# Group 3's query transposes moved from TensorE to the DMA crossbar, its queries loaded ahead of its keys

## The chip, the cores and the metric

The kernel runs on one core of one Trainium2 chip. The metric is the time of one execution on the device in microseconds (us). TensorE is called PE below, VectorE DVE, ScalarE ACT, GpSimd POOL and SyncE SP, as in the profile.

## The reference

Windowed attention with four "sink" tokens, and behind it a gated feed-forward block on the same tokens:

```
scores = scale * q @ k.T                  # 4 batches, 8 heads, 768 tokens, head size 64
keep   = (key < 4) | (0 <= query - key < 128)
a      = softmax(where(keep, scores, -1e9))
x      = (a @ v) as 3072 tokens x 512
out    = (silu(x @ w_gate) * (x @ w_val)) @ w_out     # 512 -> 1536 -> 512
```

## The kernel before

**Tiling.** The 3,072 tokens are twelve groups of 256, three to a batch; group g is batch g // 3. Group 3 is thus the first group of the second batch. For attention, PE needs keys and queries with the head dimension along the partitions (tiles kT and qT, one of each per batch), while HBM holds them with tokens first, so each group's keys and queries have to be turned. `load_nat(g)` (line 106) loads them untouched into a tile `nat[g]` of 128 partitions, with four DMAs that POOL issues at line 113: two for the keys and then two for the queries, each 128 tokens by 512. Two routes turn such a block of 128 x 512:

- `step_TN(g, i, j, evict)` (line 273): four transposes on PE at line 279 into a PSUM tile `pn`, and one copy from there into kT or qT (i = 0 or 1) for token block j, by ACT (line 283) or DVE (line 285).
- `xbar(g, which)` (line 287): one DMA transpose a block at line 293, issued by SP, from `nat[g]` straight into kT or qT.

Group 2 and group 3 go by PE, groups 4 to 11 by the crossbar. Groups from 4 on share one single-buffered tile for `nat`; group 3's lies in a pool of three.

**The feed-forward** runs over eight token blocks tb of 256 or 512 tokens. A `gate` unit (line 611) is a projection into `pg` (line 564), a tanh on ACT (584), a projection into `pv` (564), and two DVE operations (592, and 598, 603 or 607). A `down` unit (line 644) is the last product into `pd` (657). They read xT, the turned attention output, which groups from 3 on get from another DMA transpose that SP issues (`step_X`, line 538).

**What sets the order.** The order is written out by hand: `weave` walks a list of units, and a dictionary hangs attention steps on them by the unit's number. In a `gate` unit, a step marked `ahead` stands before `pg`, and the others stand between `pg` and `pv`. Every engine takes its own instructions in that order. In the list that the change touches (from line 860), units 12 to 17 are the six gates of token block 2 and units 18 to 23 the downs of blocks 0 to 2. On it hang, among others: group 4's loads at unit 11; group 3's four `step_TN` at units 14 and 15; `xbar(4)` and group 5's loads at unit 15; group 3's scores (`S1(3)`, matmuls at line 382, the first readers of its kT and qT, marked ahead) at unit 17; group 3's PV products and group 4's scores at units 19 and 20, with the keys of `xbar(5)` and xT of group 3 on SP; then the rest of `xbar(5)` and xT of group 4.

**Queues.** SP issues, in this order: eight small loads `vcl` of sink values (line 211), the four transposes of `xbar(4)`, two of `xbar(5)`, two for xT of group 3, two of `xbar(5)`, two for xT of group 4. Every DMA issued by SP or ACT takes the next of eight semaphores in turn, and waits until the one that used that semaphore eight places before has landed; POOL's DMAs have eight of their own. POOL issues group 3's loads long before (they are in its program behind all the weights), then group 4's keys, queries and values, and group 5's once `xbar(4)` has landed, since that reads the single `nat` buffer.

Of the kernel before, what the change touches and what calls it, by code (L numbers as in the profile page):

```python
# [14 lines left out]
def kernel(  # L15
# [90 lines left out]
    def load_nat(g):  # L106
        b, c = divmod(g, GC)
        x = (natp if g > 3 else rowp).tile(
            [P, 2, 2, DM], BF16, tag="nat" if g > 3 else "rows", name="nat")
        for i, src in ((0, k), (1, q)):  # L110
            for j in range(2):
                t0 = c * 256 + j * P
                nc.gpsimd.dma_start(  # L113
                    x[:, i, j].rearrange("p (h d) -> p h d", d=D),
                    src[b, :, t0:t0 + P].rearrange("h p d -> p h d"))
        nats[g] = x
# [556 lines left out]
    def A(fn, *a):  # L673
        return lambda: fn(*a)

    def TN(g, evict="av"):
        return [A(step_TN, g, i, j, evict) for j in range(2) for i in range(2)]
# [126 lines left out]
    load_gate(2)  # L804
    step_vsb(0)
    load_nat(2)
    load_gate(3)
    load_v(2)
    load_gate(4)
    load_gate(5)  # L810
    for i in range(4):
        load_out(i)
    load_nat(3)
    load_v(3)
    nc.gpsimd.memset(vcl, 0.0)
# [41 lines left out]
    def NV(g):  # L857
        return L(A(load_nat, g), A(load_v, g))
# [3 lines left out]
        ((8, 8), PVs(2)[:2]), (9, [A(step_PV, 2, 0, 1, "a"), A(step_PV, 2, 1, 1, "a")]),  # L862
        ((10, 11), [A(step_X, 2, 0, "a"), ahead(A(step_X, 2, 1, "a"))]),
        (11, [NV(4), lambda: nc.gpsimd.tensor_copy(out=vcl[64:128], in_=vcl[0:64])]),
        ((14, 14, 15, 15), TN(3, "aa")),
        (15, [A(xbar, 4)]), (15, [A(load_nat, 5)]), (19, [A(xbar, 5, (0,))]),
        *one(17, 3), (18, [A(step_ks, 1)]), (18, [A(step_vsb, 1)]),
        ((19, 19, 19, 20), PVs(3)), (19, [S1(4)]), (20, [L(A(step_S2, 4), A(step_S3, 4))]), (20, Xs(3)), (20, [A(xbar, 5, (1,))]),
# [56 lines left out]
```

## Time and profile before

| | us |
|---|---|
| median of 3 runs | 233.52 (232.6 to 233.66) |
| the profiled execution | 233.03 |
| its span, first to last instruction | 231.2 |
| PE busy in the span | 226.0 (98%) |
| DVE, ACT, POOL busy | 151.1, 106.3, 84.8 |
| granted TensorE clock, mean | 1.000 |

The span is followed by engine. Where PE is busy all the time, whatever it no longer has to do comes off the time, and whatever it has to wait for is added. DMAs have no engine row of their own: an issue shows on the queue that made it (SPq, POOL), and its landing where the next instruction stops waiting. All positions below are in us from the span's start. "Landing" is the time of a DMA's last semaphore update in the trace.

### The profile page before, as it was taken

The page shows a single profiled execution, that of the slowest core. Times are in us where ns is not written, and L with a number is a line of the kernel's source. Part 1 is how long each engine was busy: PE and PEld are TensorE (multiplying, and loading weights), DVE is VectorE, ACT ScalarE, POOL GpSimd, SP SyncE. Part 2 cuts the span into 40 slices and gives each one's busy share as a digit, 9 for nine tenths or more (in the row PEclk, how much of TensorE's full clock was granted, in tenths as well). Part 3 has the DMA queues.
Part 4 walks back from the last instruction along what each step waited for, and adds up shares of the span by engine and source line. Part 5 has one row for each costly group of instructions (what it writes and reads, how often), then busy time and mean ns, then how long its engine had stood idle before and what let it go on. Part 6 is the DMA issues. An engine that isn't in the chain of part 4 may idle for free.

```text
span 231.2 us, 5467 instructions
## 1 busy us (share of the span) xinstructions
PE 226.0 (98%) x2171; PEld 126.8 (55%) x2171; DVE 151.1 (65%) x327; ACT 106.3 (46%) x212; POOL 84.8 (37%) x123
## 2 busy tenths in 40 slices
PE   7989999999999999999999999999999999999994
PEld 3669545786556854455454454454454544487443
DVE  5898888767650797960897960697960599778000
ACT  4784496367523827323626412735512823333221
POOL 8997965960500906904526064362000000000000
PEclk9999999999999999999999999999999999999999
DMA  7999999999998998998999999989814102000132
GB/s 134 164 188 178 179 199 206 163 155 125 154 168 211 80 132 103 145 197 124 134 124 118 147 87 203 144 107 131 94 48 136 48 0 45 3 0 0 69 116 91
DMA packets 112008, 28.04 MB, mean 121 GB/s; under 512 B 99056, under 2 KB 109040, under 8 KB 111984
## 3 DMA queue, kind: packets, MB, share of 16 engines
q0 software_dynamic: 79904, 14.29, 80.7%
q1 hardware_dynamic: 30672, 11.58, 28.5%
q10 hardware_dynamic: 1408, 1.84, 2.8%
q8 instruction: 17, 0.28, 0.5%
q14 instruction: 7, 0.06, 0.1%
HBM read 29.13 MB, written 6.29 MB: 153 GB/s over the span
## 4 chain that ended last, share of the span: by engine, by line
PE 93%; DMA 4%; DVE 1%; ACTq 0%; ACT 0%; issue 0%
PE pg L564 27%; PE pv L564 27%; PE pd L657 27%; PE o L494 3%; PE s L382 3%; DMA wg<-in_moe_w_gate_dram 3%; DMA st<-in_q_dram 2%; PE o L463 1%; PE pn L279 1%; PE o L454 1%; PE pk L432 1%; PE s L326 0%; PE px L543 0%; DVE kT L755 0%; PE pt L746 0%; PE s L765 0%
## 5 line engine op out<-in xcount | busy, mean ns | idle before, releaser
L592 DVE SCALAR_TENSOR_TENSOR u<-th,pg 128x512 bf16<-128x512 f32 x72 | 49.1, 683 | 45.3 <-ACT th L584 44.9
L564 PE MATMUL pg<-xT,wg 128*128 128x512 bf16 (+1 forms) x368 | 74.2, 333 | 0.5 <-DMA wg<-in_moe_w_gate_dram 0.5
L564 PE MATMUL pv<-xT,wv 128*128 128x512 bf16 (+1 forms) x368 | 74.1, 333 | 0.0
L584 ACT ACTIVATE th<-pg 128x512 f32<-128x512 f32 x72 | 43.8, 608 | 59.4 <-PE pg L564 59.2
L657 PE MATMUL pd<-wo,ht 128*128 128x512 bf16 (+2 forms) x300 | 65.9, 370 | 0.0
L564 PEld LDWEIGHTS <-wg 128*128 128x128 bf16 x368 | 35.2, 98 | 26.5 <-DMA wg<-in_moe_w_gate_dram 0.7
L564 PEld LDWEIGHTS <-wv 128*128 128x128 bf16 x368 | 34.6, 98 | 22.8 <-issue 0.2
L607 DVE TENSOR_TENSOR ht<-u,pv 128x512 bf16<-128x512 bf16 x60 | 41.2, 686 | 4.5 <-PE pv L564 0.4
L657 PEld LDWEIGHTS <-ht 128*128 128x128 bf16 x300 | 27.6, 98 | 28.4
L662 ACT ACTIVATE ot<-pd 128x512 f32<-128x512 f32 (+1 forms) x24 | 14.3, 595 | 50.2 <-PE pd L657 50.2
L395 ACT ACTIVATE e<-s 128x512 bf16<-128x512 f32 x54 | 28.5, 614 | 5.8 <-PE s L382 5.4
L113 POOL DMA_DIRECT2D nat<-in_k_dram x20 | 17.8, 896 | 28.6 <-DMA qT<-nat 27.1
L511 DVE TENSOR_TENSOR xn<-o,rcp 128x256 bf16<-128x256 f32 x45 | 17.9, 420 | 0.7
L128 POOL DMA_DIRECT2D vm<-in_v_dram x24 | 17.8, 772 | 1.1 <-DMA va<-in_v_dram 0.8
L113 POOL DMA_DIRECT2D nat<-in_q_dram x20 | 17.8, 908 | 1.0 <-DMA wg<-in_moe_w_gate_dram 0.8
L494 PEld LDWEIGHTS <-e 128*128 128x128 bf16 x256 | 11.5, 98 | 6.0 <-issue 0.2
L404 DVE TENSOR_TENSOR e<-e,maskq 128x768 bf16<-128x768 bf16 x24 | 13.1, 552 | 1.9 <-ACT e L395 1.9
L151 POOL DMA_DIRECT2D va<-in_v_dram x12 | 10.7, 921 | 4.5 <-DMA wo<-in_moe_w_out_dram 2.5
L703 POOL CAST warmed<-xT 1x1 f32<-1x1 bf16 x3 | 0.5, 175 | 28.5 <-DMA xT<-xn 28.5
L503 DVE RECIPROCAL rcp<-o 128x4 f32<-128x4 f32 x48 | 7.1, 171 | 4.8 <-PE o L494 4.5
L664 DVE TENSOR_SCALAR ot<-pd 128x128 f32<-128x128 f32 x1 | 0.3, 292 | 14.3 <-PE pd L657 14.3
L333 ACT ACTIVATE e<-s 128x512 bf16<-128x512 f32 x16 | 8.3, 625 | 0.3 <-PE s L326 0.3
(86 smaller groups left out, 141.4 us busy)
## 6 DMA issues: line engine op xcount, KB each, us to landing
out_dram<-ot SPq DMA_DIRECT2D x17, 256.0 KB
nat<-in_k_dram POOLq DMA_DIRECT2D x20, 128.0 KB, 4.2
nat<-in_q_dram POOLq DMA_DIRECT2D x20, 128.0 KB, 5.2
va<-in_v_dram POOLq DMA_DIRECT2D x12, 128.0 KB, 5.5
wg<-in_moe_w_gate_dram POOLq DMA_DIRECT2D x6, 256.0 KB, 7.1
wv<-in_moe_w_val_dram POOLq DMA_DIRECT2D x6, 256.0 KB, 7.6
wo<-in_moe_w_out_dram POOLq DMA_DIRECT2D x4, 384.0 KB, 11.1
out_dram<-ot ACTq DMA_DIRECT2D x6, 256.0 KB
```

The source lines that it names most:

```text
L113: nc.gpsimd.dma_start(x[:, i, j].rearrange("p (h d) -> p h d", d=D), src[b, :, t0:t0 + P].rearrange("h p d -> p h d"))
L128: nc.gpsimd.dma_start(vms[b][p0:p1, t - 1, :, 0:D], v[b, :, t0:t0 + p1 - p0].rearrange("h p d -> p h d"))
L395: nc.scalar.activation(e_t[g][:, e0:e0 + 512], pss[g][w, i], AF.Exp, scale=scale)
L404: nc.vector.tensor_tensor(e, e, m.broadcast_to([P, 2, 384]), op=ALU.mult)
L494: nc.tensor.matmul(o, l, r, start=(c == 0 and i == 0), stop=(i == len(mms) - 1), skip_group_check=True)
L511: nc.vector.tensor_tensor(xn, po[:, :, 0:D], rcp.broadcast_to([P, 4, D]), op=ALU.mult)
L564: nc.tensor.matmul(ps[:, i * n:(i + 1) * n], ws[fi][:, c, fo * P:(fo + 1) * P], xTs[tb][:, c], start=(c == 0), stop=(c == DMC - 1))
L584: nc.scalar.activation(th, pg, AF.Tanh, scale=0.5)
L592: nc.vector.scalar_tensor_tensor(u, th, 1.0, pg, op0=ALU.add, op1=ALU.mult)
L607: nc.vector.tensor_tensor(hts[tb][:, f:f + 512 // SIZES[tb]].rearrange("p a n -> p (a n)"), u, pv, op=ALU.mult)
L657: nc.tensor.matmul(po, hts[tb][:, f, ts * P:(ts + 1) * P], wos[f // n][:, f % n, lo:hi], start=(f == 0), stop=(f == DFC - 1))
L662: nc.scalar.activation(ot, po, AF.Copy, scale=0.5)
```

## The change

`load_nat(3)` loads the two query blocks first and the two key blocks behind them; all other groups keep keys first. On the list of units, group 3's queries go by `xbar(3, (1,))`, hung on unit 12, so SP issues their two DMA transposes ahead of `xbar(4)`. PE keeps the keys: one `step_TN` in unit 14 and one in unit 15, evicted by ACT. The order of instructions of the two kernels differs in nothing else: PE has 8 transposes fewer (4,344 to 4,328 rows, loads of weights counted), ACT two copies fewer, POOL two pairs of loads exchanged, SP two transposes more between `vcl` and `xbar(4)`.

```diff
@@ load_nat
-        for i, src in ((0, k), (1, q)):
+        for i, src in (((1, q), (0, k)) if g == 3 else ((0, k), (1, q))):
@@ the list of units
-        ((14, 14, 15, 15), TN(3, "aa")),
+        (12, [A(xbar, 3, (1,))]), ((14, 15), [A(step_TN, 3, 0, j, "aa") for j in range(2)]),
         (15, [A(xbar, 4)]), (15, [A(load_nat, 5)]), (19, [A(xbar, 5, (0,))]),
```

## The prediction

> **What bounds the kernel now.** I read the page first: the span is 231.2 us and PE is busy through all of it.
>
> ```profile
> span 231.2 us, 5467 instructions
> PE 226.0 (98%) x2171; PEld 126.8 (55%) x2171; DVE 151.1 (65%) x327; ACT 106.3 (46%) x212; POOL 84.8 (37%) x123
> PE   7989999999999999999999999999999999999994
> ```
>
> So PE work that goes comes off the time, and any wait of PE is added whole. Next I read the chain of work that ended last around group 3's transposes (start, us, what):
>
> ```profile
> 45.53 0.87 PE pg L564 x8
> 46.41 0.45 PE pn L279 x8
> ...
> 48.60 0.45 PE pn L279 x8
> ...
> 51.67 0.77 PE s L382 x18
> ```
>
> PE goes from one to the next without a gap: the longest idle of PE behind the first 16 us is under 0.15 us. The two rows of `pn` are the sixteen transposes of group 3, 0.45 us for each eight. The row `s` is S1(3), the first reader of what they made. Third is the timeline of SP, which has to make the queries instead, and what it waited for from 44 to 58 us (total, times, longest):
>
> ```profile
> 40.65 2.67 SPq L211 DMA_DIRECT2D vcl<-in_v_dram  x8
> 49.52 2.58 SPq L293 DMA_TRANSPOSE kT<-nat  x2
> 52.20 2.52 SPq L293 DMA_TRANSPOSE qT<-nat  x2
> ```
>
> ```profile
> SPq L293 <- DMA nat<-in_k_dram: 3.9, 1, 3.9
> SPq L293 <- DMA vcl<-in_v_dram: 2.3, 1, 2.3
> ```
>
> SP is free at 43.3, waits 2.3 us for the first of the `vcl` loads to land (45.62, by its semaphore), and 3.9 us more for group 4's keys. Last, the DMA engines from 45 to 55 us, in 40 slices of 0.25 us:
>
> ```profile
> DMA  9999999999999999999999999999999999999999
> GB/s 157 151 177 150 156 210 148 146 145 145 154 155 152 155 155 153 154 154 156 151 151 157 152 153 149 152 156 174 187 153 122 100 107 68 84 159 148 174 246 179
> ```
>
> They are full: POOL's loads of values and of group 4 stand in a backlog. From about 51.75 to 53.5 the bytes fall from 150 to 68 GB/s: that is `xbar(4)`'s first transpose running beside that backlog.
>
> **The change, part by part.**
>
> *PE.* Eight transposes go: 8 x 0.056 = 0.45 us (one row of eight). All of it is on the path, none beside other PE work. PE reaches S1(3) at 51.60 (its first matmul) - 0.45 = 51.15. Removed with them are two ACT copies of 0.605 us; ACT is busy 46% and no PE wait in this stretch ends at it, so I count them at nothing; nor can they give more, as PE has no idle time here.
>
> *Order of the loads.* POOL issues the same four loads at the same times, so the queries take the first places. By the semaphores those land at 43.54 and 44.51 and the other two at 45.47 and 46.34. The keys now take the latter; PE reads the first at 46.14 (unit 14) and the second at 48.2 (unit 15), 0.7 and 1.9 us late enough. Cost: nothing; if the first landed over 0.7 us later, the excess.
>
> *When SP issues.* The two new transposes stand behind `vcl`. The first needs the query block (43.54) and the semaphore of the first `vcl` load (45.62), so it goes at 45.64. An issue takes 1.22 to 1.27 us, so the second goes at about 46.95, and SP is free at 48.2, ahead of the 49.52 at which group 4's keys let `xbar(4)` begin. SP's own time thus delays nothing; if those keys came sooner, at most the 2.5 us of two issues.
>
> *When they land.* No transpose runs at 46 us before, so the duration comes from others. From issue to the last semaphore update: 2.45 us with nothing beside it (69.97 to 72.42). Pairs that met POOL's backlog (issue of the first, landing of the second, difference; POOL's packets beside each):
>
> ```
>  81.40 ->  87.28   5.88   2365, 1108   (the backlog ends in between)
>  49.52 ->  55.76   6.24   4538, 2863
>  94.96 -> 101.85   6.89   4391, 4131
> 110.91 -> 118.23   7.32   4356, 2648
> 123.22 -> 131.93   8.71   4792, 3334
> 142.47 -> 150.12   7.65   2372, 3061
> 155.65 -> 162.83   7.18   4297, 2707
> ```
>
> The backlog at 45.6 is as thick as in the last six (about 600 of POOL's packets each 0.5 us) and has nine more us to run. So I take their median, 7.25 us: the second lands at 45.64 + 7.25 = 52.89. S1(3) waits for both. PE stands 52.89 - 51.15 = **1.74 us**. The bounds: 5.88 gives a wait of 0.37; 8.71, and 1.0 more because the `vcl` loads are ahead on the same queue until 48.60, gives 4.2. What stands behind the waiting matmul is all of PE's work, so everything shifts by the same. Net so far: 1.74 - 0.45 = +1.29.
>
> *What the transposes cost POOL's loads.* In the dips at 52, 97, 99 and 126 us POOL's queue falls short of its rate by 0.7 to 1.15 us for each transpose that runs beside it; alone, a transpose takes 0.5 us (`xbar(4)` lands at 55.12, 55.76, 56.24 and 56.72, once the backlog is gone). Two more cost 1.0 to 2.3 us; I take 2 x 0.9 = 1.8. So `xbar(4)` lands at about 58.5; S1(4) needs it at 59.45 + 1.29: covered by 2.2 us. But group 5's load waits for it, and from there a tight chain runs: group 5's keys, two transposes, two for xT of group 3, two more, two for xT of group 4, all back to back on SP from 61.98 to 73.84. POOL and PE show its end:
>
> ```profile
> 57.27 1.75 POOL L113 DMA_DIRECT2D nat<-in_k_dram  x2 [6.22 <-DMA qT<-nat]
> ...
> 75.32 0.18 POOL L703 CAST warmed<-xT 1x1 f32<-1x1 bf16 x1 [14.54 <-DMA xT<-xn]
> ```
>
> xT of group 4 lands at 75.26, and PE reads it at 75.72: 0.46 us of cover. Late by 1.8, it comes at 77.06; PE, late by 1.29, asks at 77.01. That adds 0.05. Behind it the next link is group 6's queries (88.32, read at 89.15: 0.83 of cover), and from 103 us on xT and kT land 2 us and more ahead, so no more is added.
>
> **Sum:** 233.03 (the profiled execution: 231.2 of span and 1.8 around it) - 0.45 + 1.74 + 0.05 = **234.4 us**, +0.6%. The profiled execution lies 0.49 under the median of the runs; against that median the same sum would be 234.9, inside the range.
>
> **A rule against the change.** One transpose of 128 x 128 on PE costs 0.056 us of the path here, and its crossbar counterpart has 2.45 us as its shortest row. [...]
>
> **The rivals.**
>
> 1. *A short wait at S1(3), and xT of group 4 as the end.* If the pair lands as early as the shortest contended row, the wait is 0.37 and PE asks for xT at 75.64. With 1.0 to 1.8 us of delay it lands at 76.26 to 77.06: a wait of 0.6 to 1.4, and 233.6 to 234.4 us. For it: the order of waits is a matter of one us. Against it: six of seven contended pairs took longer. Chance 0.26.
> 2. *In time (not slower).* If the transposes run as without a backlog, the second lands at 46.95 + 2.45 = 49.4, 1.7 us ahead of PE. The point from which this holds is a pair in under 5.5 us. Then the time is 233.03 - 0.45 = 232.6, or up to 233.6 if POOL's loads still lose 1.0. For it: the rows without a backlog. Against it: no pair beside a backlog was that quick. Chance 0.14. [...]
> 3. *A long wait.* `vcl` ahead on the queue and a pair like that at 123 us: 55.4, a wait of 4.2, net +3.75, 236.8 us. Chance 0.08.
>
> **How the numbers follow.** The forecast has the remaining 0.52, with its own spread of about 234.2 to 235.5. A measurement of this kernel can tell about 0.5% (1.17 us) from no change. The forecast and the long wait lie nearly all above +1.17 (0.57 of 0.60); the short wait and in time nearly all within (0.40, with what the forecast leaves); no mechanism here gives more than 0.45 us back, so faster by over 0.5% has 0.02, for chance alone; slower 0.57, within 0.41. The range leaves out half of the long waits and most of "in time": 232.8 to 236.1.
>
> **What would show it.** In the changed kernel: two rows of `pn` with 0.22 us each; SP's new pair at 45.6 and 46.9; PE idle ahead of S1(3), released by DMA qT<-nat, at about 51.1 to 52.9; group 5's load at about 59 in place of 57.27; POOL's row for xT near 77. No idle at S1(3) makes the landing step wrong; idle there with no shift of group 5's load makes the cost to POOL's loads wrong; a wait at `pn` makes the loads' order wrong.

## The result: 2.8% slower

| | before | changed |
|---|---|---|
| median of 6 runs each, us | 233.18 (232.60 to 233.89) | 239.72 (238.83 to 240.52) |
| the profiled execution, us | 233.03 | 240.52 |
| its span, us | 231.2 | 238.7 |
| granted clock, mean over the span of the profiled execution | 1.000 | 0.986 |

The ratio is 1.0277, with a 95% interval of 1.0245 to 1.0310: +6.5 us between the medians. The forecast was 234.4 and its range ended at 236.1; the sign was right and the size was not.

The changed kernel's page shows a gap in PE's row that the kernel before has nowhere, and beside it something that no view of before had: a slice in which the granted clock, the share of its full rate that TensorE is given, is 5 tenths.

```profile
span 238.7 us, 5454 instructions
...
PE   7979999975999999999999999999999999999994
...
PEclk9999999995899999999999999999999999999999
```

The same row of the kernel before:

```profile
PEclk9999999999999999999999999999999999999999
```

The other five executions of the changed kernel have mean clocks of 0.984 to 0.993, so each of them had such a stretch too, whose place is not seen without a trace.

What ended PE's waits, over the whole span (total, times, longest; the second line is the start of the kernel, where PE went on 1.2 us later than in the profile of before; the kernels start alike, and in most of the other profiles this wait is 0.5 to 1.2 us):

```profile
PE s L382 <- DMA qT<-nat: 3.7, 1, 3.7
PE pg L564 <- DMA wg<-in_moe_w_gate_dram: 1.5, 1, 1.5
```

In the kernel before, the second line reads as follows, and the first has no counterpart:

```profile
PE pg L564 <- DMA wg<-in_moe_w_gate_dram: 0.5, 1, 0.5
```

The chain of work through this place (start, us, what), and the same stretch by stages (length, PE busy, then the other engines, granted clock, DMA share, GB/s):

```profile
48.12 7.89 DMA qT<-nat
56.00 0.14 issue
56.14 1.46 PE s L382 x18
57.60 1.82 PE pg L564 x8
59.42 1.71 PE pv L564 x8
61.13 3.74 PE pd L657 x16
```

```profile
52.00:54.50 2.50, 0.41 (x4) 0.12 (x2) 1.37 (x2) 0.17 (x1) 0.00 (x0) 1.00 2.71 138
54.80:56.10 1.30, 0.00 (x0) 0.00 (x0) 0.00 (x0) 0.00 (x0) 0.00 (x0) 0.50 2.02 150
56.20:61.50 5.30, 5.30 (x36) 3.67 (x37) 1.41 (x3) 3.62 (x7) 0.64 (x1) 0.50 0.94 88
61.70:65.00 3.30, 3.30 (x20) 1.58 (x19) 2.38 (x7) 0.60 (x1) 2.66 (x4) 1.00 1.26 80
```

The second transpose was issued at 48.12 and landed at 56.00; PE had stood since 52.42. When it went on, S1(3) took 1.46 us where it had taken 0.77, and the `pg` behind it 1.82 where it had taken 0.98: nearly twice as long. The stage from 56.2 to 61.5 shows why. PE is busy all of it at a clock of 0.50, and a busy row alone would not have told it. The clock records put the half clock from 54.77 to 61.59, 6.83 us, of which 5.45 had work to do.

Matched matmul by matmul, the two profiles differ by +1.24 us ahead of group 3 (the start), then -0.45 for the transposes (`pn` is now eight matmuls), +3.72 for the wait, +2.6 until the clock is back at 61.6, and nothing that grows behind that: together 7.1 of the 7.5 us between the spans, the rest standing behind the last matmul. Without the start that is 5.9, against 6.5 between the medians.

SP and POOL of the changed kernel:

```profile
46.71 2.61 SPq L293 DMA_TRANSPOSE qT<-nat  x2
49.74 2.60 SPq L293 DMA_TRANSPOSE kT<-nat  x2
52.44 3.16 SPq L293 DMA_TRANSPOSE qT<-nat  x2
```

```profile
60.86 1.75 POOL L113 DMA_DIRECT2D nat<-in_k_dram  x2 [9.58 <-DMA qT<-nat]
```

SP's new pair goes out first, as the list of units says, and its own issues delay the next ones by nothing (49.74 is when group 4's keys landed). Group 5's load goes 3.6 us later than before (60.86 for 57.27); 1.1 us of that is the later start, as POOL's first load of group 4 goes at 43.32 for 42.23.

### The profile page after: what moved, and what is told of

It reads as the page before. It is cut to its first block, busy times and chain, and to the rows that moved or that the text cites. A ratio compares the mean times of both kernels' runs of the same rounds, so it can differ in the third digit from the quotient of the medians.

```text
span 238.7 us, 5454 instructions
## 1 busy us (share of the span) xinstructions
PE 228.4 (96%) x2163; PEld 127.9 (54%) x2163; DVE 151.6 (63%) x327; ACT 105.7 (44%) x210; POOL 84.3 (35%) x123
## 4 chain that ended last, share of the span: by engine, by line
PE 78%; DMA 17%; POOL 1%; DVE 1%; issue 1%; SPq 1%; POOLq 0%
PE pd L657 26%; PE pg L564 21%; PE pv L564 20%; DMA wv<-in_moe_w_val_dram 7%; DMA wo<-in_moe_w_out_dram 4%; PE s L382 3%; DMA qT<-nat 3%; PE o L494 2%; DMA vcl<-in_v_dram 2%; PE w L730 1%; PE o L463 1%; PE pt L746 1%; PE pk L432 1%; SPq L293 1%; PE o L454 1%
## 5 line engine op out<-in xcount | busy, mean ns | idle before, releaser
L564 PE MATMUL pg<-xT,wg 128*128 128x512 bf16 (+1 forms) x368 | 75.0, 336 | 1.5 <-DMA wg<-in_moe_w_gate_dram 1.5
L564 PE MATMUL pv<-xT,wv 128*128 128x512 bf16 (+1 forms) x368 | 75.0, 336 | 0.0
L564 PEld LDWEIGHTS <-wv 128*128 128x128 bf16 x368 | 35.1, 99 | 23.1 <-issue 0.2
L395 ACT ACTIVATE e<-s 128x512 bf16<-128x512 f32 x54 | 28.5, 610 | 9.8 <-PE s L382 9.4
L494 PEld LDWEIGHTS <-e 128*128 128x128 bf16 x256 | 11.6, 98 | 6.1 <-issue 0.2
L382 PE MATMUL s<-qT,kT 64*64 64x64 bf16 (+4 forms) x366 | 8.5, 223 | 3.7 <-DMA qT<-nat 3.7
L382 PEld LDWEIGHTS <-kT 64*64 64x64 bf16 (+1 forms) x366 | 6.8, 108 | 7.3 <-issue 7.2
```

Of the source, the lines that this page charges most:

```text
L382: nc.tensor.matmul(pss[g][w, lo // 8][part, 64 * (lo % 8):64 * (lo % 8) + 64 * (hi - lo)], kTs[b][r, p, k0:k0 + kn], qTs[b][r, p, cc:cc + ...
L395: nc.scalar.activation(e_t[g][:, e0:e0 + 512], pss[g][w, i], AF.Exp, scale=scale)
L494: nc.tensor.matmul(o, l, r, start=(c == 0 and i == 0), stop=(i == len(mms) - 1), skip_group_check=True)
L564: nc.tensor.matmul(ps[:, i * n:(i + 1) * n], ws[fi][:, c, fo * P:(fo + 1) * P], xTs[tb][:, c], start=(c == 0), stop=(c == DMC - 1))
```

## The experiments

**Theory.** The loss is (a) the wait at S1(3), long because the transposes run beside POOL's backlog of loads, and (b) the half clock that came behind that wait (0.50 from 54.77 to 61.59), which the prediction had not priced. **Rivals:** the new order of the loads; the place behind `vcl` on SP; the delay of group 4's and 5's loads, with no part of the wait; transposes that are slow by themselves. The ratio of each kernel to before is given with its 95% interval.

**1. The order of the loads alone.** The kernel before with this line of the change:

```diff
-        for i, src in ((0, k), (1, q)):
+        for i, src in (((1, q), (0, k)) if g == 3 else ((0, k), (1, q))):
```

> Group 3's queries are loaded ahead of its keys, and PE turns both as before. If the order of the loads costs nothing, the time is that of before, 233.2 within 0.5. If the order is what costs (keys late for unit 14, or a shift in POOL's queue), PE waits at pn and the time goes towards 239.7.

Measured: 233.05 us beside 233.29, ratio 0.999 (0.996 to 1.001), and no PE wait at `pn`. The order costs nothing.

**2. The transposes without the wait.** As 1, and:

```diff
+        (12, [lambda: [nc.sync.dma_start_transpose(scratch[:, j], nats[3][:, 1, j]) for j in range(2)]]),
         ((14, 14, 15, 15), TN(3, "aa")),
```

> As e1_order, and SP also makes the two crossbar transposes of group 3's queries, at unit 12, into a tile that nothing reads: their DMA cost without a PE wait for them. If the cost is the wait at S1(3) and the slow clock behind it alone, 233.2. If it is the delay of POOL's loads and of the chain behind them (group 5's load at about 60 in place of 57.3, xT of group 4 about 2 to 3 us later than PE asks for it), 235 to 236, with an idle PE at about 75.7. If even the transposes' mere presence gives the whole loss, 239.7.

Measured: 236.15 beside 233.29, ratio 1.012 (1.006 to 1.018), full clock in the profile. S1(3) starts at 51.47, on time. The first transpose was issued at 45.59 and the second landed at 55.68. PE and POOL later; the first line is S1(5) in the kernel before, which does not wait:

```profile
74.58 0.89 PE L382 MATMUL s<-qT,kT 64*64 64x192 bf16 x52
```

```profile
75.91 0.83 PE L382 MATMUL s<-qT,kT 64*64 64x192 bf16 x45 [1.15 <-DMA qT<-nat]
```

```profile
91.94 0.84 PE L382 MATMUL s<-qT,kT 64*128 64x256 bf16 x18 [1.40 <-DVE ht L607]
```

```profile
60.15 1.75 POOL L113 DMA_DIRECT2D nat<-in_k_dram  x2 [8.94 <-DMA qT<-nat]
```

The two PE rows that wait are S1(5) and S1(6). Group 5's load is late by 2.9 us, its queries land at 75.78 (3.4 us late: 1.9 by the issue of the last transpose, 1.4 by its length), and group 6's at 91.80 (the profile names DVE for the second, but that had long been done; POOL's `turned(6)`, a step that waits for the same queries, is released at 91.92). So two transposes in this stretch cost 2.9 us even if nobody waits for them. In the changed kernel this cost is not seen, because PE is late by more: group 5's queries land at 76.20 there, and S1(5) starts at 81.72.

**3. PE kept busy through the wait.**

```diff
+        (17, [ahead(lambda: fill(17, bank([P, 512], FP32, "w"), 512))]),
         *one(17, 3),
```

> The changed kernel with 17 matmuls of 512 columns on zeros put ahead of S1(3), about 3.7 us of PE work in the place of the wait. The wait stays covered but costs its time. If the slow clock behind the idle stretch is a cost of its own, it is gone: granted clock 1.000 and 233.2 - 0.45 + 3.7 = 236.5. If the clock is a mark and no cost, 239.7 as the changed kernel.

Measured: 237.22 beside 233.29, ratio 1.016 (1.011 to 1.021). The wait is covered: the second block lands at 54.95, S1(3) starts at 55.08.

```profile
51.14 3.83 PE L730 MATMUL w<-zero 128*128 128x512 bf16 x17
55.08 0.84 PE L382 MATMUL s<-qT,kT 64*128 64x256 bf16 x18
```

```profile
55.00:60.00 5.00, 4.92 (x46) 3.32 (x47) 2.41 (x5) 3.54 (x7) 0.00 (x0) 1.00 1.38 113
60.00:65.00 5.00, 5.00 (x97) 2.87 (x96) 3.73 (x12) 2.17 (x5) 3.51 (x4) 1.00 0.91 100
```

With the same DMAs and nearly the same delay but no idle PE, the clock stays at 1.00 and the loss is 3.9 us in place of 6.5: the half clock is a cost of its own, some 2.6 us. Work of no use on PE made the changed kernel faster.

**4. `vcl` behind the transposes.**

```diff
-    load_sinks(vcl, 1, B)
...
-        (11, [NV(4), lambda: nc.gpsimd.tensor_copy(out=vcl[64:128], in_=vcl[0:64])]),
-        (12, [A(xbar, 3, (1,))]),
+        (11, [NV(4)]),
+        (12, [A(xbar, 3, (1,)), A(load_sinks, vcl, 1, B), lambda: nc.gpsimd.tensor_copy(out=vcl[64:128], in_=vcl[0:64])]),
```

> The changed kernel with the eight small vcl loads put behind the two transposes on SP, so that these go as soon as the queries have landed, about 2 us sooner. If the place behind vcl makes them late, they land in time: 232.8, no idle at S1(3). If the backlog of POOL's loads makes them slow, they still take 7 to 9 us from the first issue to the second landing, and PE waits about 1 to 2 us: 234 to 235 with the clock held, 236 to 238 if it falls all the same.

Measured: 237.36 beside 233.29, ratio 1.017 (1.011 to 1.023). Issued at 43.98, the pair lands at 53.20: 9.2 us again, so the place behind `vcl` is not what makes it long. The same length begun sooner leaves PE a wait of 1.61 us at S1(3), and there are 0.35 and 1.75 more at S1(4) and S1(5), in the profile:

```profile
PE s L382 <- DMA qT<-nat: 3.7, 3, 1.8
```

The profiled execution held the clock (mean 0.998) and took 237.38, over the forecast of 234 to 235 for that case by 2 us: the waits at S1(4) and S1(5) had been left out of it. The edit is part of their cause, since the `vcl` loads now stand ahead of `xbar(4)`, which SP issues at 53.57 in place of 49.74. The other three executions, with mean clocks of 0.986 to 0.992, took 237.16 to 238.44.

**5. The backlog taken away.** Group 4's loads (`NV(4)`: keys, queries and values) are held on POOL until the two transposes have landed, for which `turned(3)` waits.

```diff
-        (11, [NV(4), lambda: nc.gpsimd.tensor_copy(out=vcl[64:128], in_=vcl[0:64])]),
-        (12, [A(xbar, 3, (1,))]),
+        (11, [lambda: nc.gpsimd.tensor_copy(out=vcl[64:128], in_=vcl[0:64])]),
+        (12, [A(xbar, 3, (1,)), A(turned, 3), NV(4)]),
```

> The changed kernel with all of group 4's loads held on POOL until the two transposes have landed, so that these meet only group 3's last loads. If POOL's backlog makes the pair slow, it lands by about 51 (under 6 us in place of 9.3) and PE waits at S1(3) for 0.5 us at most, at full clock; group 4 is then late instead, with waits of 1 to 2 us at S1(4) and S1(5), 235 to 236. If the pair is slow by itself, the wait of 3.7 us and the slow clock stay, and the time is 239.7 or more.

Measured: 241.74 beside 233.65, ratio 1.035 (1.032 to 1.039). The pair is issued at 45.99 and 47.72 and lands at 49.47 and 50.20, the second in 2.48 us. S1(3) does not wait (first line below; the second is S1(4)):

```profile
51.60 0.84 PE L382 MATMUL s<-qT,kT 64*128 64x256 bf16 x18
```

```profile
65.71 1.50 PE L382 MATMUL s<-qT,kT 64*64 64x192 bf16 x52 [6.18 <-DMA qT<-nat]
```

So the backlog is what makes the pair long; the time is worse, since S1(4) then waits 6.18 us and the clock falls there (its 52 matmuls take 1.50 us for 0.89 before; mean clock 0.986). The forecast of 1 to 2 us for that wait was wrong: held until 50.5, group 4's loads ran beside its own four transposes, of which the first went at 53.81 for 49.52 before and the last landed at 65.57 for 56.72.

**6. A shorter gap.** As 3, with five of the matmuls.

```diff
-        (17, [ahead(lambda: fill(17, bank([P, 512], FP32, "w"), 512))]),
+        (17, [ahead(lambda: fill(5, bank([P, 512], FP32, "w"), 512))]),
```

> The changed kernel with 5 of the matmuls on zeros ahead of S1(3), so about 2.6 us of idle PE are left of 3.7. If the clock falls some 2.4 us after PE has stopped, as in the changed kernel's profile, it falls, and the time is about 239 to 239.7. If it takes an idle stretch of over 2.6 us, it holds, and the time is that with 17 of them, 237.2.

Measured: 238.92 (three runs: 239.04, 238.92, 237.03) beside 233.65, ratio 1.020 (1.016 to 1.025). In the profile PE stood 3.23 us, as the pair was longer than expected, and the clock fell 3.0 us after PE had stopped, for 3.41 us. The mean clock is 0.991 and 0.993 in the two runs at 239 and 0.998 in the run at 237.03.

**7. Early.** Group 3's loads stand ahead of the output weights on POOL, its transposes ahead of `vcl` on SP.

```diff
     load_gate(5)
+    load_nat(3)
     for i in range(4):
         load_out(i)
-    load_nat(3)
...
+    xbar(3, (1,))
     load_sinks(vcl, 1, B)
...
-        (12, [A(xbar, 3, (1,))]), ((14, 15)
+        ((14, 15)
```

> The changed kernel with group 3's loads ahead of the output weights' on POOL, and its two transposes ahead of vcl on SP: they go at about 38 to 39 and may take 9 us without PE waiting. If the wait and the clock were all, 232.8 (0.45 under before). If the two transposes also delay POOL's loads for group 4 and, through the single nat buffer, group 5 by about 2.9 us, waits of 1 to 1.5 us at S1(5) and S1(6) stay: 235 to 236.

Measured: 235.70 beside 233.65, ratio 1.009 (1.006 to 1.012). The pair is issued at 36.11 and lands at 47.61, 3.8 us ahead of S1(3), which does not wait. Group 5's load is late by 2.35 us. Its last query transpose goes 1.1 us later than before (71.06 for 69.97), and takes 5.33 us in place of 2.45, with four stores of the output in flight beside it in place of two; S1(5) waits:

```profile
76.53 0.89 PE L382 MATMUL s<-qT,kT 64*64 64x192 bf16 x52 [2.02 <-DMA qT<-nat]
```

**8. Early, and a buffer of its own for group 5.**

```diff
-        x = (natp if g > 3 else rowp).tile(
-            [P, 2, 2, DM], BF16, tag="nat" if g > 3 else "rows", name="nat")
+        own = g in (2, 3, 5)
+        x = (rowp if own else natp).tile([P, 2, 2, DM], BF16, tag="rows" if own else "nat", name="nat")
```

> As e8_early, and group 5 is loaded into a free buffer of group 3's pool, so that its load need not wait until xbar(4) has landed. If that wait is the path by which the delay reaches PE, the waits at S1(5) and S1(6) go: 232.8, or 0.2% under before. If the transposes slow whatever stands in the backlog, group 5's load just joins it, and 234 to 236 remains.

Measured: five runs of 235.89 (the profiled one), 237.00, 237.98, 239.47 and 240.09, at mean clocks of 1.000, 0.993, 0.993, 0.986 and 0.986; ratio 1.014 (1.010 to 1.018) for the three quickest. Group 5's load goes at 55.07 with no wait for a landing, and S1(5) and S1(6) do not wait. But its packets now stand beside `xbar(4)`, whose last transpose lands at 61.82 in place of 56.72, and S1(4) waits:

```profile
61.95 0.89 PE L382 MATMUL s<-qT,kT 64*64 64x192 bf16 x52 [2.53 <-DMA qT<-nat]
```

The wait moved; it did not go.

**9. Group 4's values out of the backlog**: in the early kernel, in the kernel before as a control, and in the changed kernel.

```diff
-        (11, [NV(4), lambda: nc.gpsimd.tensor_copy(out=vcl[64:128], in_=vcl[0:64])]),
+        (11, [A(load_nat, 4), lambda: nc.gpsimd.tensor_copy(out=vcl[64:128], in_=vcl[0:64])]),
...
-        (15, [A(load_nat, 5)]),
+        (15, [A(load_nat, 5), A(load_v, 4)]),
```

> As e8_early, and group 4's five value loads stand behind group 5's keys and queries on POOL, so they wait until xbar(4) has landed and are no part of the backlog that it meets. If that backlog is what makes group 5 late, xbar(4) lands by about 57, group 5's queries are there when S1(5) asks, and the values (asked for at 64.3) are in time by a little: 232.8 to 233.5. If any two more transposes here cost their time whatever stands around them, a wait of 1 to 2 us at S1(5) stays: 235 to 236; if the values come late, the wait moves to the PV products of group 4.

> The kernel before with that one shift of group 4's value loads: the control for e13. Nothing of before waits in this stretch, so 233.4 as before, or later if the values do not come in time for group 4's PV products.

> The changed kernel with the same shift: the two transposes of group 3 meet group 4's keys and queries, but no values behind them. If their length follows the backlog beside them, the pair lands at about 53 in place of 55 to 56, PE waits 1.5 to 2.5 us, and the time is 235 to 237.5, depending on the clock. If it does not depend on it, 239.7.

Measured: 244.81, 241.87 and 241.98 beside 233.19; ratios 1.050 (1.045 to 1.054), 1.035 (1.031 to 1.038), 1.036 (1.031 to 1.040). All three lose at the values, which land at 71 to 72.5, while PE was ready for them at 65 to 66; the third kernel's waits:

```profile
PE o L463 <- DMA vm<-in_v_dram: 5.1, 3, 2.4
PE s L382 <- DMA qT<-nat: 1.5, 1, 1.5
```

As versions they are useless, and no forecast gave a time for late values; two had named them as a possibility. The control says that the shift alone costs 8.7 us of the 8.8 to 11.6. As measurements they serve. Without a backlog beside it, `xbar(4)` of the early kernel lands each transpose 2.42 to 2.46 us after its issue. And in the third kernel group 3's pair, which meets group 4's keys and queries but not its values, takes 7.27 us (45.47 to 52.74) in place of 9.29.

**10. One block of two.**

```diff
-        (12, [A(xbar, 3, (1,))]), ((14, 15), [A(step_TN, 3, 0, j, "aa") for j in range(2)]),
+        (12, [lambda: nc.sync.dma_start_transpose((new_T(1), qTs[1])[1][:, :, 0:P], nats[3][:, 1, 0])]),
+        ((14, 15, 15), [A(step_TN, 3, 0, 0, "aa"), A(step_TN, 3, 0, 1, "aa"), A(step_TN, 3, 1, 1, "aa")]),
```

> Half of the change: only the first query block goes by the crossbar, PE turns the second with four transposes more than the changed kernel. One transpose beside the backlog took 6.5 to 7.3 us as the first of a pair: it lands at about 52 to 53, PE (0.22 us early) waits 0.7 to 1.8 us at full clock, 234 to 235. If one alone is no slower than without a backlog, no wait and 233.1.

Measured: 235.42 beside 233.19, ratio 1.010 (1.006 to 1.014). One transpose alone beside the backlog took 7.33 us (45.95 to 53.27), and PE waited 2.36 us in the profile, more than the forecast of 0.7 to 1.8:

```profile
53.41 0.84 PE L382 MATMUL s<-qT,kT 64*128 64x256 bf16 x18 [2.36 <-DMA qT<-nat]
```

That run had the half clock for 3.41 us and took 236.46; two others at full clock took 235.42 and 235.30.

**Together.** The pair's length against POOL's packets that passed beside its first and second transpose:

```
kernel                         packets      issue of first to landing of second, us
5, loads held                   906,   21    4.2
9, changed, values late        5412, 3039    7.3
3, PE filled                   6029, 5604    8.6
4, vcl behind                  6426, 7164    9.2
changed                        5802, 5527    9.3
6, five matmuls                7063, 5289    9.6
2, spare                       7468, 5367   10.1
7, early                       2580, 2704   11.5
```

The packets are counted while the transposes run, so a longer pair sees more of them pass: the table alone does not show the cause, but the kernels that took loads away, 5 and 9, do. Nor is the number of packets the whole measure: the early pair of experiment 7 had the fewest but one beside it and took the longest. Most of its bytes are the output weights', in packets of 1,024 bytes in place of 128: 1.4 and 1.6 MB passed beside its two transposes, against 0.73 and 0.69 MB in the changed kernel.

No kernel tried here beats the one before. Those that took the wait at S1(3) away by an earlier issue or an emptier queue found it again at S1(4), S1(5), S1(6) or the values, for more than the 0.45 us to be won.

## Why the prediction was wrong

**Right:** the 0.45 us of PE (`pn` went from two rows of 0.45 to eight matmuls in all); the order of the loads at nothing (experiment 1); SP's issues at nothing; the place of the new wait, S1(3), its releaser, and that all of it is added. The direction had a chance of 0.57.

**The first step that failed is "When they land".** The prediction took the median of six pairs in the kernel before, 7.25 us, and a wait of 1.74. The pair took 9.29 and the wait was 3.72. The reading beneath it, a backlog "as thick as in the last six" rows, was wrong, and the trace of before could have told it. From 45.6 us on, 9,081 of POOL's packets still had to pass there before its queue ran dry (over half a us without one) at 54.8, the nine us that the prediction itself named. From the start of the rows at 49 to 156 us it was 2,368 to 5,691, and the pair at 142 us met none at its start. The sum should have lengthened the rows for a backlog about twice as large instead of taking their middle. Experiments 5 and 9 show that dependence (4.2 and 7.3 us with less in the queue), and 4 shows that the `vcl` loads, which the upper bound blamed, have no part in it. This step alone gives 233.03 - 0.45 + 3.72 = 236.3, just past the end of the range. The long wait was on the list, with 4.2 us and 236.8, at a chance of 0.08.

**The second is a term that the sum did not have: the clock.** The prediction priced a PE wait at its own length. The trace of before could not show otherwise: its clock is 1.000 and its longest idle of PE 1.2 us, at the start. Here the half clock took 2.6 us more (experiment 3). With it, the long wait alone comes to -0.45 + 3.72 + 2.6 = 5.9, 2.8 us past the end of the range. The half clock lasted 6.83 us here and 3.41 in experiments 6, 7 and 10. It came with shorter waits than this one too, 2.02 us in experiment 7 and 2.36 in 10, while one of 2.53 in experiment 8 had none (mean clock 1.000).

**The third is the size and the place of the delay behind.** The prediction gave POOL's loads 1.8 us of delay, to be felt first at xT of group 4. Alone it is 2.9 us (experiment 2), and what comes late first is group 5's queries, which the prediction had not checked (they land at 72.42 before and S1(5) starts at 74.58: 2.2 us of cover), and then group 6's. In the changed kernel PE's own lateness hid it, so this error cost nothing in the sum; it has a part in the waits that stop the cures of experiments 4 and 7.

**Open:** 0.6 us between the parts from the profile (5.9) and the medians (6.5), and as much again between the sum for experiment 3 (236.5) and its time (237.2); why the clock fell with the wait of 2.02 us in experiment 7 and not with the one of 2.53 in experiment 8 (last section); and how the crossbar and POOL's loads hinder each other inside the DMA engines, of which only the rates were seen.

## What to carry to other kernels

With PE as the bound (98% busy), four transposes on it cost 0.22 us of the path here, and a crossbar transpose costs none only if it lands before its reader asks and the loads that it pushes back have that much room: the pair of experiment 7 landed 3.8 us ahead of S1(3), pushed group 5's load back by 2.35, and the time was 235.70 for 233.65. Before moving work there, look at how much is queued beside it at that time, and lengthen the duration for it: here the pair took from 4.2 us with almost nothing beside it to 11.5. A wait that stops PE may not be priced at its length alone: waits of 2.02, 2.36, 3.23 and 3.72 us came with a half clock here, in experiments 7, 10 and 6 and in the changed kernel. So look in the stage behind a wait for the granted clock, and if there must be one, matmuls on zeros can be the cheaper way to spend it, as in experiment 3 (ratio 1.016 in place of 1.028).

## What the runs showed of the hardware

- A DMA transpose of 128 x 512 landed 2.4 to 2.5 us after its issue with nothing, or next to nothing, beside it (2.45 in the kernel before, 2.48 in experiment 5, 2.42 to 2.46 in the early kernel of experiment 9). Those of group 3's queries issued at 44 to 48 us beside the full queue of loads took 6.5 to 8.8 us, one alone (7.33) as long as either of two; the early pair beside the weights took 8.1 and 10.1. With none of POOL's loads beside it, but four stores of the output, one took 5.33 (experiment 7); that the stores are the cause was not tested. The loads pay as well: two such transposes made group 5's load 2.9 us late (experiment 2).
- The granted clock was 0.50 for a while behind some of PE's waits and not behind others. In the changed kernel PE stood 3.72 us from 52.42 on, and the clock was at half from 54.77 to 61.59. A wait of 3.23 us (experiment 6) and one of 2.36 us (10) came with 3.41 us at half clock each. So did the 2.02 us of experiment 7: the mean clock is 0.73 from 75 to 80 us and 0.93 from 80 to 85 there, and the fall came 0.76 us after PE had gone on. With the 2.53 us of experiment 8 the mean clock of the whole execution is 1.000, and with the waits of 1.61 and 1.75 us in experiment 4 it is 0.998.
- So the length of a wait did not tell by itself whether the clock fell: 2.02 us lost it and 2.53 us kept it. What decides between them was not shown. The same kernel had the half clock in some executions and not in others (experiment 10: means of 0.993, 1.000, 1.000), but those others have no trace. Executions of the kernel before have mean clocks of 0.985 to 1.000 as well.
- At half clock PE's row reads busy all the time (5.30 us of 5.30 at a clock of 0.50 in the changed kernel): the cost showed only in the duration of the matmuls (18 of S1(3) in 1.46 us for 0.77 before) and in the granted clock of the stage.
